# Attention with beacon keys and a low-rank token mixer on one core: the first batch's masks put on TensorE, half of its loads cast by the DMA, its mixing and first products cut into pieces

## The chip, the cores and the metric

The kernel runs on one core of one Trainium2 chip. The metric is the device time of one execution in microseconds (us). A core has TensorE (PE in the profile; its weight loads are PEld), VectorE (DVE), ScalarE (ACT), GpSimd (POOL) and SyncE (SP), which run beside each other and wait for one another by semaphores. DMA transfers are issued from the queues of SP, ACT or POOL.

## The reference, cut to what matters

There are 8 batches of 8 heads, 576 tokens, head size 64, and 16 beacon keys and values per head that every token may see. The output of the attention, 576 x 512 per batch, goes through a low-rank mixing over the tokens (rank 32) and a channel network of width 2048.

```python
k_all = concat([beacon_k, k], axis=2); v_all = concat([beacon_v, v], axis=2)
scores = (q @ k_all^T) / 8                      # q: 8, 8, 576, 64; k_all: 8, 8, 592, 64
scores[t, 16 + s] = -1e9 where s > t            # causal; the 16 beacons are always seen
x = softmax(scores) @ v_all                     # heads laid side by side: 8, 576, 512
u = x + (U @ V mixing over tokens of x)         # h = x^T @ U @ V; u = x + h^T
out = u + relu(u @ w_ch1) @ w_ch2
```

## The kernel before, in words

Heads are worked in pairs: pair p is heads 2c and 2c + 1 of batch b, with p = 4b + c, so pairs 0 to 3 are the first batch. The output tokens of all batches, 4608, are cut into nine blocks of 512 for the channel network.

The program is a list of steps in a string, SCRIPT (L855), that `step` (L791) takes one by one; each engine gets its instructions in that order and takes them strictly in it. The names of the steps that matter here:

- `I1`: one keep-warm matmul of the identity on 128x512 (L241), whose result is not used. `Sa0:3` has three of them ahead of the score step.
- `k`, `q`, `b`, `v`: loads of a batch, or of its half A or B (heads 0 to 3, 4 to 7), issued from POOL (L190 to L204), which cast f32 to f16 on the way. `w10` to `w13` and `w20`, `w21` load the weights of the network in quarters and halves, from POOL too (L180, L185). `u` loads U and V from SP.
- `GkV0`: regroup k (or q) of a pair for the transposes, on V (DVE), A (ACT) or G (POOL) (L253). `HkV0`: copy the first 80 rows of a pair, f32 to f16 (L743). `TqV1`: five transposes on PE and two copies from PSUM (L261 to L265).
- `Sa0` to `Sd0`: the four score groups of a pair. PE multiplies (L316; the two heads of a pair lie in the two halves of the array's rows, 64 each), ACT takes exp (L321).
- `M0.0`, `M0.1`: the mask of a head. DVE takes the minimum of exp and a mask that is 65504 where a key is seen and 0 where it is not (L304, L306). `B` fills the larger mask (L118 to L122).
- `A0.0`: one head's values on PE (L331, 15 matmuls), reciprocal and product on DVE (L339, L340).
- `X0.0` to `X0.2`: the mixing of batch 0 over all four blocks of 128 channels: a head (L371, 20 matmuls, then a copy to f16 on DVE) and two parts (transposes L390, closing matmuls of 32 rows L397, copies on ACT and DVE L406, L408). In the later batches the transposes come from DMA.
- `g0.9`: the first layer of block 0, 128 of its 2048 columns: four matmuls of 512 columns (L529), one for each 128 channels, then relu on ACT, and for the lower half on ACT and DVE (L533 to L539).
- `P02.0` and others: products of the second layer (L620), in an arrangement with seven products per block in place of eight; `p00.0` are sums for them, `W0` sums of weights, `U0.0` transposes by DMA.

All of PSUM is one pool of eight banks (L102), which the steps take in turn. POOL holds the waits for its transfers itself: it issues one after the other.

At the start, `load_first` (L691) brings all of q and k of the first batch as f32 into two staging tiles, pair by pair: pair 0's q from ACT's queue, the rest from SP's. Regroup and head copies then cast to f16. The later batches come by POOL, already cast. The stage that the change touches is the first 200 steps of SCRIPT, up to `X1.0` and `v2`; it holds pairs 0 to 7, the mixing of batch 0, the first layer of block 0, and the start of the second batch's mixing.

Of the kernel before, what the change touches and what calls it, by code (L numbers as in the profile page):

```python
# [27 lines left out]
def kernel(  # L28
# [269 lines left out]
    def score_units(c, qT, kT, ex):  # L298
# [11 lines left out]
        def visit(g, idle=0):  # L310
            ps = [pst([P, 512], F32, name=f"sps{i}") for i in range(2)]
            keep_warm(ps[0], idle)
            for ch, qa, w, o in groups[g]:
                for i in range(2):
                    hp = slice(D * i, D * i + D)
                    nc.tensor.matmul(  # L316
                        ps[i][:, ds(o, w)], kT[hp, c, ds(P * ch, P)], qT[hp, c, ds(qa, w)],
                        start=True, stop=True,
                    )
# [35 lines left out]
    def mix_units(xb, u0, xt=None, shifted=True):  # L355
# [10 lines left out]
        def head():  # L366

            qtp = pst([P, P], F32, name="qtp")
            for m, j in rows:
                for cc in range(NCC):  # L370
# [9 lines left out]
        def part(a, e):  # L380
            n = e - a
            ups = [pst([P, n], F32, name="ups") for _ in range(NCC)]
            if xt is None:
                for cc in range(NCC):
# [10 lines left out]
            for cc in range(NCC):  # L395
# [5 lines left out]
            for cc in range(NCC):  # L401
# [8 lines left out]
        return head, [lambda a=a, e=e: part(a, e) for a, e in zip(cuts, cuts[1:])]  # L410
# [99 lines left out]
    def block_steps(t, dst):  # L510
# [11 lines left out]

        def g_unit(dc):
# [3 lines left out]
            g = pst([P, 512], F32, name="gps")  # L527
            for cc in range(NCC):
                nc.tensor.matmul(  # L529
                    g, w1[:, cc, ts(dc, P)], uT[:, cc, ds(ring(t0), 512)], start=(cc == 0), stop=(cc == NCC - 1)  # L530
                )
# [202 lines left out]
    def group(p, i, copy):  # L734
# [3 lines left out]
        regroup(Ls[b], c, i, copy, prs[p])  # L738
        if b == 0 and not any(t[0] == "H" and t[1] == "kq"[i] and t[3:] == str(p) for t in SCRIPT.split()):
# [51 lines left out]
    def step(t):  # L791
# [7 lines left out]
        elif name in "kqbv":  # L799
# [56 lines left out]
        HqA0 I1 GkA0 I1 I1 I1 GqA0 I1 I1 HkV0 u I1 I1 I1 GkV1 I1 B I1 I1 I1 TqA0 TkA0 I1 TkV1 I1 s v0A  # L856
# [174 lines left out]
```

## Time and profile before

| | |
|---|---|
| median of 3 runs | 339.12 us (338.91 to 340.06) |
| the profiled execution | 339.2 us |
| its span, first to last instruction | 337.5 us |
| mean granted TensorE clock | 0.998 |
| busy: PE, DVE, ACT, POOL | 327.8, 264.8, 228.0, 99.3 us |
| bytes moved by DMA | 44.17 MB, mean 131 GB/s |
| exp on ACT (L321), 256 of them | 111.6 us |
| first-layer matmuls (L529), 384 of them | 91.8 us |
| masks on DVE (L304), 64 of them | 26.7 us |

A row of the timeline or of a group names the line, the engine, the operation, the tiles written and read, the shape and the count; behind the bar or in brackets stands the time that the engine was idle just before, and what released it. The chain of waits is followed back from the last instruction: at each step to what released it, or to the instruction before it on its engine. PE's busy time has modelled ends, so a busy PE says that it had work, not that it ran at its peak.

### The profile page before, as it was taken

How to read it: one execution, taken by the hardware profiler on the slowest of the kernel's cores; microseconds unless marked ns; L12 is line 12 of the kernel's file. 1: busy time of each engine (PE TensorE's matmuls, PEld its weight loads, DVE VectorE, ACT ScalarE, POOL GpSimd, SP SyncE). 2: the span in 40 equal slices, each digit the busy share in tenths (PEclk: the TensorE clock that was granted, in tenths of full speed). 3: DMA queues.
4: the chain of work that ended last, by engine and by line, in shares of the span. 5: the costliest groups of instructions: out<-in, count | busy, mean ns of one | idle time of the engine just before them, and what ended most of it. 6: DMA issues, size and time to landing. Idle time of an engine off the chain costs nothing.

```text
span 337.5 us, 8954 instructions
## 1 busy us (share of the span) xinstructions
PE 327.8 (97%) x3527; PEld 228.0 (68%) x3527; DVE 264.8 (78%) x690; ACT 228.0 (68%) x494; POOL 99.3 (29%) x129
## 2 busy tenths in 40 slices
PE   7989999999999999999999999999999999999994
PEld 3446466765678655766577547765688888888883
DVE  2888588985778757875888868886999999896882
ACT  4897898749778889878785799267912842644500
POOL 9765662340621602450024410000002503303300
PEclk9999999999999999999999999999999999999999
DMA  9999999999999999999979997554545501203042
GB/s 178 221 196 196 153 167 195 98 168 175 164 180 176 169 188 150 124 136 187 189 109 145 172 183 96 83 114 100 51 62 161 93 2 63 80 0 95 3 113 98
DMA packets 136145, 44.17 MB, mean 131 GB/s; under 512 B 108417, under 2 KB 131969, under 8 KB 136097
## 3 DMA queue, kind: packets, MB, share of 16 engines
q0 software_dynamic: 69008, 17.54, 61.3%
q1 hardware_dynamic: 66496, 25.66, 42.0%
q8 instruction: 29, 0.48, 0.6%
q10 hardware_dynamic: 592, 0.34, 0.3%
q14 instruction: 20, 0.16, 0.2%
HBM read 37.63 MB, written 9.44 MB: 139 GB/s over the span
## 4 chain that ended last, share of the span: by engine, by line
PE 75%; DVE 16%; DMA 3%; issue 3%; ACT 2%; SPq 0%; DVEq 0%; ACTq 0%
PE gps L529 23%; PE cpY L620 15%; PE po L331 8%; PE sps L316 8%; PE cpD L620 7%; PE cpA L620 3%; PE fpY L566 3%; DMA stm<-in_q_dram 3%; DVE gT L581 3%; DVE sT L601 2%; DVE ob L645 2%; DVE uT L404 2%; PE fpD L566 2%; PE tps L263 1%; ACT expt L321 1%
## 5 line engine op out<-in xcount | busy, mean ns | idle before, releaser
L321 ACT ACTIVATE expt<-sps 128x496 f16<-128x496 f32 (+2 forms) x256 | 111.6, 538 | 15.8 <-PE sps L316 14.3
L529 PE MATMUL gps<-uT,w 128*128 128x512 f16 x384 | 91.8, 379 | 0.0
L620 PEld LDWEIGHTS <-gT 128*128 128x128 f16 x576 | 54.6, 98 | 10.5 <-issue 2.2
L529 PEld LDWEIGHTS <-w 128*128 128x128 f16 x384 | 34.3, 98 | 37.4 <-issue 2.5
L587 POOL TENSOR_SCALAR gT<-gT 128x512 f16<-128x512 f16 x12 | 17.8, 1495 | 105.6 <-DVE gT L581 89.0
L620 PEld LDWEIGHTS <-sT 128*128 128x128 f16 x432 | 41.0, 98 | 7.8 <-issue 2.0
L331 PEld LDWEIGHTS <-expt 128*128 128x128 f16 (+1 forms) x960 | 35.5, 98 | 9.2 <-DVE expt L304 1.3
L203 POOL DMA_DIRECT2D vs<-in_v_dram x50 | 40.5, 825 | 3.2 <-DMA w<-in_moe_w_ch_dram 2.5
L539 ACT ACTIVATE gT<-gps 128x512 f16<-128x512 f32 x48 | 29.8, 630 | 15.5 <-PE gps L529 15.2
L304 DVE TENSOR_TENSOR expt<-expt,bigmask 128x512 f16<-128x512 f16 x64 | 26.7, 417 | 17.2 <-ACT expt L321 17.2
L331 PE MATMUL po<-vs,expt 128*128 128x65 f16 (+1 forms) x960 | 38.0, 194 | 1.0 <-ACT expt L321 1.0
L620 PE MATMUL cpY<-wsum,gT 128*128 128x256 f16 x288 | 36.1, 273 | 0.0
L620 PE MATMUL cpD<-w,sT 128*128 128x256 f16 x288 | 35.5, 273 | 0.3 <-DVE sT L601 0.3
L316 PE MATMUL sps<-qT,kT 64*128 64x80 f16 (+4 forms) x384 | 34.5, 282 | 0.4 <-ACT kT L109 0.3
L340 DVE TENSOR_TENSOR xb<-po,rec 128x320 f16<-128x320 f32 x64 | 31.5, 492 | 2.2
L534 DVE SCALAR_TENSOR_TENSOR gT<-gps,gT 128x256 f16<-128x256 f32 x48 | 19.8, 420 | 14.9 <-ACT gT L533 14.8
L109 ACT ACTIVATE hP<-fpY 128x512 f32<-128x512 f32 x24 | 13.7, 598 | 23.0 <-PE fpY L566 18.8
L533 ACT ACTIVATE gT<-gps 128x256 f16<-128x256 f32 x48 | 19.5, 418 | 11.5 <-PE gps L529 11.0
L316 PEld LDWEIGHTS <-kT 64*128 64x128 f16 x384 | 13.9, 94 | 18.7 <-issue 10.1
L645 DVE TENSOR_TENSOR ob<-cpY,ut 128x512 f32<-128x512 f32 (+1 forms) x28 | 18.7, 667 | 6.0 <-PE cpY L620 6.0
L566 PEld LDWEIGHTS <-wf 128*128 128x128 f16 x192 | 18.6, 98 | 3.0 <-issue 0.7
L620 PE MATMUL cpY<-w,gT 128*128 128x256 f16 x144 | 17.7, 273 | 0.0
(115 smaller groups left out, 477.6 us busy)
## 6 DMA issues: line engine op xcount, KB each, us to landing
out_dram<-ob SPq DMA_DIRECT2D x16, 512.0 KB, 4.5
st<-in_k_dram POOLq DMA_DIRECT2D x6, 512.0 KB, 8.9
st<-in_q_dram POOLq DMA_DIRECT2D x6, 512.0 KB, 8.6
vs<-in_v_dram POOLq DMA_DIRECT2D x18, 128.0 KB, 7.7
w<-in_moe_w_ch_dram POOLq DMA_DIRECT2D x4, 512.0 KB, 8.6
w<-in_moe_w_ch_dram POOLq DMA_DIRECT2D x2, 1024.0 KB, 12.6
stm<-in_k_dram SPq DMA_DIRECT2D x4, 256.0 KB, 5.0
stm<-in_q_dram SPq DMA_DIRECT2D x3, 256.0 KB, 5.6
```

The source lines that it names most:

```text
L203: nc.gpsimd.dma_start(out=dst[a : a + nq[j], j, :, :], in_=src[hs, ds(q0[j], nq[j]), :].rearrange("h p d -> p h d"))
L304: nc.vector.tensor_tensor(out=e4, in0=e4, in1=bigmask, op=ALU.min)
L316: nc.tensor.matmul(ps[i][:, ds(o, w)], kT[hp, c, ds(P * ch, P)], qT[hp, c, ds(qa, w)], start=True, stop=True,)
L321: nc.scalar.activation(out=ex[i][:, ds(PAD + SLOT * g, gw[g])], in_=ps[i][:, 0 : gw[g]], func=AF.Exp, scale=scale)
L331: nc.tensor.matmul(po[:, j, :], ex[0 : nk[c], ds(blk[(c, j)], P)], vs[0 : nk[c], ds(c * H * E + h * E, E)], start=(c == 0), stop=(c == j),)
L340: nc.vector.tensor_tensor(out=xb[:, h // 2, :, ds(D * (h % 2), D)], in0=po[:, :, 0:D], in1=r.broadcast_to([P, NT, D]), op=ALU.mult)
L529: nc.tensor.matmul(g, w1[:, cc, ts(dc, P)], uT[:, cc, ds(ring(t0), 512)], start=(cc == 0), stop=(cc == NCC - 1))
L534: nc.vector.scalar_tensor_tensor(out=gT[:, dc, H2:512], in0=g[:, H2:512], scalar=0.0, in1=gT[:, dc, 0:H2], op0=ALU.max, op1=ALU.subtract,)
L539: nc.scalar.activation(out=gT[:, dc, :], in_=g, func=AF.Relu)
L566: nc.tensor.matmul(ps[:, i, :], a[:, kk, ts(2 * mp + i, P)], b[:, kk, :], start=opens and i == 0 and kk == 0, stop=kk == 1, skip_group_che ...
L620: nc.tensor.matmul(ps[:, i, :], a[:, f, ds(P * i, P)], b[:, f, :], start=opens and i == 0 and f == 0, stop=f == NK - 1, skip_group_check=True,
L645: nc.vector.tensor_tensor(out=out, in0=ps[:, ii, :], in1=other, op=ALU.add)
```

## The change

The first batch's masks go from DVE to PE. Two operands are filled once at the start (`fill_masks`): `sel` has 65504 times the identity in two halves, `nm` has 0 where a key is seen and -65504 where it is not. Their product, -65504 squared at the masked places, is added to the scores in PSUM ahead of exp, so that exp gives 0 there. The steps `M0` to `M3` go. `B` comes later, since only pairs 4 and up use the old mask.

Pairs 2 and 3 are no longer loaded as f32 by SP: the steps `q0B`, `k0B` and `b0B` load them from POOL as f16, and their head copies go. SP and ACT load pairs 0 and 1.

The mixing of batch 0 is done per block of 128 channels: `D1.0` is the head of block 1, `D1.1` and `D1.2` are its parts. The first-layer products of six column groups are split: `E0.8` does the first three blocks of 128 channels, and `g0.8` the last.

The order of the stage is another. 25 keep-warms stand ahead of the first transpose, where 13 stood; there are 36 in the stage in both. Behind `v2` the list is the same.

```diff
+    msk = outp.tile([P, 2, 2, P], F16, name="msk", tag="ob")
+    sel, nm = msk[:, 0], msk[:, 1]
+    HP = P // 2
+    def fill_masks():
+        nc.vector.memset(sel, 0.0)
+        nc.vector.memset(nm[:, 1, 0:HP], -F16_MAX)
+        nc.vector.memset(nm[:, 0, HP:P], 0.0)
+        for i in range(2):
+            r = slice(HP * i, HP * i + HP)
+            for h in range(2):
+                nc.vector.tensor_scalar(
+                    out=sel[r, h, ds(HP * h, HP)], in0=ident[r, r], scalar1=F16_MAX, scalar2=None, op0=ALU.mult
+                )
+                nc.vector.tensor_scalar(
+                    out=nm[r, h, ds(HP * h, HP)], in0=mask[r, r], scalar1=F16_MAX, scalar2=None, op0=ALU.subtract
+                )
...
-    def score_units(c, qT, kT, ex):
+    def score_units(c, qT, kT, ex, masked=False):
...
-                        start=True, stop=True,
+                        start=True, stop=not masked, skip_group_check=masked,
                     )
+                if masked and qa == q0[ch]:
+                    a = Nb if ch == 0 else 0
+                    for h, e in ((0, HP), (1, min(P, w))):
+                        for i in range(2):
+                            hp = slice(D * i, D * i + D)
+                            nc.tensor.matmul(
+                                ps[i][:, ds(o, e - a)], sel[hp, h, :], nm[hp, h, a:e],
+                                start=False, stop=True, skip_group_check=True,
+                            )
...
-        def head():
+        def head(ccs=range(NCC)):
...
-                for cc in range(NCC):
+                for cc in ccs:
...
-        def part(a, e):
+        def part(a, e, ccs=range(NCC)):
...
+        def g_part(dc, ccs=range(NCC - 1)):
+            if ccs[0] == 0:
+                cell["g", dc] = pst([P, 512], F32, name="gps")
+            for cc in ccs:
+                nc.tensor.matmul(
+                    cell["g", dc], w1[:, cc, ts(dc, P)], uT[:, cc, ds(ring(t0), 512)],
+                    start=(cc == 0), stop=(cc == NCC - 1), skip_group_check=True,
+                )
...
-        main = gtp.tile([P, 2, H, 4 * D], F32, name="stm", tag="gT")
-        head = gtp.tile([P, 2, H, D], F32, name="sth", tag="gT")
+        main = gtp.tile([P, 2, H // 2, 4 * D], F32, name="stm", tag="gT")
+        head = gtp.tile([P, 2, H // 2, D], F32, name="sth", tag="gT")
+        Ls[0] = qk_tiles()
...
+        main_load(nc.scalar, q[0], main[:, 1, SETS[0], :], SETS[0])
+        main_load(nc.sync, k[0], main[:, 0, SETS[0], :], SETS[0])
+        head_load(nc.scalar, q[0], head[:, 1, SETS[0], :], SETS[0], 0)
+        head_load(nc.sync, k[0], head[:, 0, SETS[0], :], SETS[0], Nb)
+        beacon_load(nc.scalar, beacon_k[0], head[:, 0, :, :], HS)
...
-        for hs in SETS[1:]:
-            kload(hs)
-            qload(nc.sync, hs)
+        main_load(nc.sync, k[0], main[:, 0, SETS[1], :], SETS[1])
+        head_load(nc.sync, k[0], head[:, 0, SETS[1], :], SETS[1], Nb)
+        main_load(nc.sync, q[0], main[:, 1, SETS[1], :], SETS[1])
+        head_load(nc.sync, q[0], head[:, 1, SETS[1], :], SETS[1], 0)
...
-        HqA0 I1 GkA0 I1 I1 I1 GqA0 I1 I1 HkV0 u I1 I1 I1 GkV1 I1 B I1 I1 I1 TqA0 TkA0 I1 TkV1 I1 s v0A
-        Sd0 Sb0 Sa0:3 I1 GqV1 TqV1 GkV2 Sc0 I1 GqV2 v0B I1 I1 Sc1 Sb1 I1 M0.0 Sd1 M0.1 TqV2 TkV2 I1 A0.0
...
+        v0A I1 q0B k0B b0B I1 I1 I1 I1 GqA0 q1A I1 I1 I1 I1 I1 I1 GkA1 I1 I1 I1 GkV0 HkV0 I1 I1 HqV0 I1 I1
+        I1 I1 u I1 I1 I1 s I1 I1 TqA0 I1 TkV0 TkV1 Sa0:3 Sb0 Sc0 GqV1 TqV1 I1 cV I1 Sd0 I1 Sa1:2 Sb1 Sc1
+        Sd1 w12 I1 v0B GqV3 eV GqV2 I1 TqA3 GkV2 GkV3 A0.0 TqV2 TkV2 TkA3 A1.0 k2 A0.1 A1.1 I1 GqA5 Sd2 Sb3
+        I1 Sa2:1 Sd3 D1.0 D0.0 D1.2 k1A b1 GqV4 Sc3 Sa3:1 Sc2 Sb2 TqV5 A3.0 D0.1 A3.1 I1 w13 TqA4 A2.0 D1.1
+        D3.0 A2.1 GkA4 D3.2 D0.2 GkV5 D2.0 D3.1 b2 D2.2 k1B GkV11 U0.0 TkV5 TkV4 D2.1 Sb5 Sd5 GkV7 E0.8 Sd4
+        g0.8 q1B g0.11 w10 GkV6 Sb4 Sa5:0 Sc4 Sc5 g0.10 B g0.13 GqV6 E0.9 TqV6 TkV6 I1 I1 v1A GqV7 g0.9
+        TkV11 Sa4 q2 M4.0 E0.0 M4.1 g0.0 GkA8 TkA7 E0.2 U0.2 M5.0 g0.2 g0.12 TkV8 A4.0 A4.1 GqV8 TqA7 A5.0
+        Sa6:0 Sb6 M5.1 Sc6 E0.3 TqV8 U0.1 E0.1 A5.1 Sd6 Sb7 g0.15 GkV10 GqV9 w11 M6.1 g0.1 g0.3 g0.7 GqV11
+        GkV9 M6.0 v1B p00.0 Sa7 Sd7 Sc7 M7.0 g0.14 M7.1 A6.1 g0.6 A6.0 Sc8 Sd8 A7.1 GqV10 A7.0 TkA9 TqA9
+        p00.2 g0.5 p00.1 w20 g0.4 Sd9 Sc9 Sa8 X1.0 w21 TqA11 v2 b3 p01.0 p01.2 X1.1 P02.0 p01.1 X1.2 W0
...
     with tc.manual_schedule(engines={ENG.PE, ENG.Activation, ENG.DVE, ENG.SP, ENG.Pool}):
         load_first()
+        fill_masks()
```

More of the change, by code (lines that the diff above doesn't have):

```diff
@@ L408, in part @@
                     nc.scalar.activation(out=dst, in_=ups[cc], func=AF.Copy)
-        return head, [lambda a=a, e=e: part(a, e) for a, e in zip(cuts, cuts[1:])]
+        return head, [lambda ccs=range(NCC), a=a, e=e: part(a, e, ccs) for a, e in zip(cuts, cuts[1:])]
     def mlp_units(t0, n, dst):
@@ L526, in g_unit @@
             gT = cell["g"]
[L527 to L531, printed above, removed]
+            if ("g", dc) not in cell:
+                g_part(dc, range(NCC))
+            else:
+                g_part(dc, range(NCC - 1, NCC))
+            g = cell["g", dc]
             if dc < NK:
@@ L737, in group @@
             prs[p] = pair_tile()
-        regroup(Ls[b], c, i, copy, prs[p])
-        if b == 0 and not any(t[0] == "H" and t[1] == "kq"[i] and t[3:] == str(p) for t in SCRIPT.split()):
+        regroup((None, raw["main"]) if p < 2 else Ls[b], c, i, copy, prs[p])
+        if p < 2 and not any(t[0] == "H" and t[1] == "kq"[i] and t[3:] == str(p) for t in SCRIPT.split()):
             first_heads(c, i, copy)
```

132 lines of the change are left out of this document (58 added, 74 removed).

## The prediction

> **What bounds the kernel now.** I read the page first, then a table of busy time by stretch, then the chain of waits of the first 62 us, then the timeline of the rows that the change touches.
>
> ```profile
> PE 327.8 (97%) x3527; PEld 228.0 (68%) x3527; DVE 264.8 (78%) x690; ACT 228.0 (68%) x494; POOL 99.3 (29%) x129
> ...
> PE   7989999999999999999999999999999999999994
> ```
>
> TensorE (PE) is busy for 97% of the span. The slices are 8.4 us each: only the first three and the last are under 9 tenths. The change rewrites 200 steps at the head of the order, the part ahead of the step `v2`; from there on both orders are the same word for word. So the question is one number: when does PE reach the end of that part?
>
> The table by stretch has, for each, the length, then the busy time of PE, weight load, DVE, ACT and POOL.
>
> ```profile
> 6.00:12.00 6.00, 5.19 (x51) 2.36 (x48) 4.57 (x21) 5.16 (x14) 5.17 (x9) 1.00 1.58 233
> 12.00:18.00 6.00, 5.72 (x77) 3.00 (x70) 5.49 (x22) 5.14 (x15) 4.69 (x8) 1.00 1.66 212
> 18.00:24.00 6.00, 4.99 (x76) 3.10 (x76) 4.76 (x19) 5.50 (x13) 3.33 (x6) 1.00 1.44 193
> 24.00:30.00 6.00, 5.53 (x80) 3.54 (x79) 5.83 (x20) 4.21 (x11) 4.57 (x7) 1.00 1.34 203
> 30.00:36.00 6.00, 6.00 (x90) 3.61 (x88) 3.88 (x12) 6.00 (x18) 2.40 (x4) 1.00 1.91 170
> 36.00:42.00 6.00, 6.00 (x38) 2.83 (x36) 3.34 (x11) 5.10 (x13) 4.95 (x7) 1.00 1.36 154
> ...
> 120.00:337.50 217.50, 211.99 (x2203) 155.27 (x2200) 174.14 (x409) 131.37 (x270) 39.30 (x40) 1.00 0.77 107
> ```
>
> PE waits only up to 30 us: 0.81 + 0.28 + 1.01 + 0.47 = 2.57 us from 6 to 30. From 30 us on it is full, and behind the stage 212 of 217.5 us. A shift at the end of the stage is therefore carried to the end one for one. DVE is the fullest engine beside PE from 12 to 30.
>
> ```profile
> 0.86 4.27 DMA stm<-in_q_dram
> ...
> 16.84 0.14 PE tps L261
> 16.98 0.23 PE tps L263 x4
> ...
> 28.24 0.22 PE idle L241
> 28.46 0.46 PE po L331 x15
> 28.93 0.32 PE sps L316 x2
> 29.24 0.32 PE idle L241
> ...
> 30.13 0.52 PE qtp L371 x20
> 30.65 0.53 PE ups L390 x8
> 31.18 0.21 PE ups L397 x4
> ...
> 31.70 0.71 PE ups L390 x12
> 32.41 0.25 PE ups L397 x4
> ...
> 33.60 0.32 PE sps L316 x6
> ...
> 35.73 6.15 PE gps L529 x28
> ...
> 43.99 0.97 PE gps L529 x4
> ...
> 46.00 0.86 PE gps L529 x4
> ...
> 59.41 0.98 PE cpA L620 x8
> ```
>
> In the chain (start, length, what) a load of q lies at the head, and behind 28 us there are rows of PE alone. The last row, at 59.41 us, is the first product of `P02.0`, just behind the common point: I take its start as the mark of the stage. The other rows are prices on PE. A transposing step T is 0.14 + 0.23 = 0.37. A keep-warm `I1` is 0.22, or 0.32 behind a score step. A value step A is 0.46, a score step `Sa` or `Sc` 0.32. The run of 28 rows at L529 gives 6.15 / 28 = 0.22 us for 512 columns, or 0.43 ns a column.
>
> **The change, part by part.** All of it is PE time up to the mark, unless I say otherwise.
>
> Keep-warms and start. Both orders have 36 `I1` and the same counts in S steps, but 25 of them now stand ahead of the first transpose, where 13 stood.
>
> ```profile
> 1.59 4.68 PE L241 MATMUL idle<-ident 128*128 128x512 f16 x13 [1.59 <-POOL ident masks.py:199]
> ...
> 4.98 0.80 PEld L241 LDWEIGHTS <-ident 128*128 128x128 f16 x4 [0.28 <-issue]
> ...
> 6.11 0.20 PE L261 MATMUL tps<-ident,hd 80*128 80x80 f16 x1
> ...
> 8.89 5.71 ACT L321 ACTIVATE expt<-sps 128x208 f16<-128x208 f32 x14 [0.35 <-PE sps L316]
> ```
>
> The first eight of the 13 take from 1.59 to 4.98, 0.42 us each; then four weight loads come in 0.80 us, (0.80 - 0.15) / 3 = 0.22 apart. Thirteen end at 6.1, where the first transpose (6.11) starts at once. Twelve more at 0.22 end at 8.7, so `TqA0` starts 2.6 us later. Nothing lets it pass them, since PE takes them in order. The same twelve are gone behind it: -12 x 0.22 = -2.6, or down to -3.2 if half of them stood behind score steps at 0.32. I take 0 in all, and -0.6 as the low end.
>
> Masks by TensorE. For pairs 0 to 3 each score step gets two matmuls per diagonal block and head: in columns, 48 + 112 for the first block, 64 + 128 for three, 64 + 80 for the last, 880 per head. The trace has no such matmul. The nearest is in the score step `Sc`: one 336-column and two 80-column matmuls per head (33.60, six rows) take 0.32, as long as one 496-column matmul per head (28.93, two rows). So the two heads run side by side on their halves of the array, and small matmuls there cost their columns only. That gives 880 x 0.43 = 0.38 a pair, 1.5 us for four; if the heads did not overlap, 3.0. No gain is possible, as nothing leaves PE here. I take 1.5, by the row that is of the same form.
>
> The Trainium skill, page "TensorE: Matmul & The Clock Gate", section "Back-to-back issue gap", would make this dearer: it says that a stream of weight load and matmul pairs is held at about 81 ns a matmul at 128 columns. By it the 80 mask matmuls would be 6.5 us, an estimate, instead of 1.5, and the sum below 5.0 higher. This trace disagrees: 15 matmuls of 65 columns with a weight load each take 0.46 us (28.46), 31 ns apiece.
>
> What the masks take off DVE lies in these groups.
>
> ```profile
> L304 DVE TENSOR_TENSOR expt<-expt,bigmask 128x512 f16<-128x512 f16 x16 | 6.6, 415 | 3.4 <-ACT expt L321 3.4
> ...
> L306 DVE TENSOR_TENSOR expt<-expt,mask 80x80 f16<-80x80 f16 x16 | 3.0, 189 | 0.0
> ...
> L159 DVE COPY one<-ident 32x32 f16<-32x32 f16 x4 | 0.6, 368 | 0.0
> ```
>
> Eight mask steps go, each 0.415 + 0.189: 4.8 us of DVE. They and the lighter regroups (f16 in place of f32) shorten what PE waited for, the 2.57 us; they are worth no more. Added are 11 small DVE instructions that fill the mask operands; by the 32 x 32 copies (0.6 us for four) about 0.15 each, 1.7 us. They lie ahead of the first loaded data (the load in the chain lands at 0.86 + 4.27 = 5.1) and cost nothing; without that cover they would delay the first copy by 1.7. The fill of the old mask moves to where DVE is busy 3.34 of 6 us.
>
> Mixing per channel block. Before, `X0` is a head (20 rows, 0.52) and two parts (0.53 + 0.21, 0.71 + 0.25). Now each is done once per block. Heads: five 128-column matmuls per block; at the 0.23 / 4 of the transposes that is 0.29 a block, 1.15 in all (+0.63), at best +0 if neighbours overlap. The four closing matmuls of a part run side by side before; alone, one of 240 columns is 240 x 0.43 = 0.10 plus what it costs to change the shape of the matmuls. That price shows in the first-layer products: four take 0.86 when value steps follow, 0.97 when 64-row scores follow, so 0.11 a change. Parts: 4 x 0.21 - 0.21 = +0.63 and 4 x 0.25 - 0.25 = +0.75 with the change, +0.20 and +0.33 without. In all +0.5 to +2.0; I take +1.4, since most of these blocks have 128-row neighbours.
>
> First-layer products split. Four of the six split products have other matmuls between their halves, two stand together. The columns are the same; a change of shape more is 0.11 each, 0 to 0.4, and I take 0.1 (only the scores between the halves of `E0.8` change it).
>
> Loads. Pairs 2 and 3 leave SP (eight issues fewer there, which lets the U and V loads go earlier) and are put on POOL, five issues ahead of the next batch's q, of `w12` and of `v0B`; `k2` moves ahead of `k1A`, and waits until pairs 2 and 3 are regrouped and transposed.
>
> ```profile
> 11.59 0.75 POOL L196 DMA_DIRECT2D st<-in_q_dram  x1 [0.83 <-DMA vs<-in_v_dram]
> ...
> 14.59 0.75 POOL L180 DMA_DIRECT2D w<-in_moe_w_ch_dram  x1 [0.25 <-DMA vs<-in_v_dram]
> ...
> 23.65 0.76 POOL L180 DMA_DIRECT2D w<-in_moe_w_ch_dram  x1 [1.61 <-DMA w<-in_moe_w_ch_dram]
> ...
> 37.33 0.76 POOL L180 DMA_DIRECT2D w<-in_moe_w_ch_dram  x1 [0.46 <-issue]
> ```
> ```profile
> w<-in_moe_w_ch_dram POOLq DMA_DIRECT2D x4, 512.0 KB, 8.6
> ...
> vs<-in_v_dram POOLq DMA_DIRECT2D x12, 64.0 KB, 7.3
> ```
>
> From the 13th issue (11.59) to the 25th (23.65) POOL needs 1.0 us each, and the row at 23.65 shows why: it waits for the weight load of 14.59, eight issues before. So five more issues are 5 us. `v0B` ends as the 20th, 11.59 + 7 = 18.6, plus 7.3 to land is 25.9; its first user, `A3.0`, comes at about 26. The last first-layer weights (`w11`) go from 37.33 to 42.3, plus 8.6 is 50.9. Its first user `g0.7` stands ahead of the mark by five g (0.9), eight S (0.28), four A, three T, and `X1` (0.4 + 0.74): 4.5 + 2.2 + 1.8 + 1.1 + 1.1 = 10.7. With the mark at 60.6 that is 49.9: possibly 1.0 late. I price the loads at 0 in the sum, 1.0 as the other end.
>
> Waits that stay. The sum so far is 0 + 1.5 + 1.4 + 0.1 = +3.0, against 2.57 us of waits that could all go: +0.4. How many stay? ACT sets the second limit. The first exp starts at 8.89 before. Now `TqA0`, `I1` and `TkV0` end at 8.7 + 0.37 + 0.22 + 0.37 = 9.6, the copies on DVE about 0.9 later, the score step 0.32 behind them: 10.9. The 14 exps from 8.89 run without a gap, 5.71 / 14 = 0.41 each; 32 of them are 13.1, with three copies of some 0.7 between them 15.2. So the last exp of pairs 0 to 3 is out at 26.1 at the earliest. PE then has about 4.4 us (two A, two T, two heads and six parts of the mixing) to the end of the mixing, and what followed that before, 59.41 - 32.66 = 26.75, plus 1.4 for work that stood ahead of it before (one T, four S) and 0.1: 26.1 + 32.7 = 58.8. PE alone gives 59.8, ACT alone 58.8. Two queues so close to full, joined by eight PSUM banks, reach neither; I keep a third of the old waits, 0.8, with 0 and 2.0 as ends.
>
> Sum: +3.0 - 2.57 + 0.8 = +1.2 us. The profiled execution took 339.2 (span 337.5 and 1.7 around it), against a median of 339.12; I count from 339.2 and get 340.4. With all low ends it is -0.6 + 1.5 + 0.5 - 2.57 = -1.2, with the high end of the mixing, of the split and of the waits +0.4 + 0.6 + 0.3 + 1.2 = +2.5 (masks at 1.5).
>
> **The rivals.** (1) No net effect: DVE was what made PE wait, and with its masks gone PE runs through. For it: 5.49 and 5.83 of 6 us in the table. Against: the first exp comes 2 us later. Time: between the +0.4 of the sum with no waits left and nothing, +0.2: 339.4. (2) Faster: as (1), and the mixing per block overlaps (+0.5, not +1.4) and the keep-warms that went were the 0.32 ones. That is the sum of low ends, -1.2: 338.0. It decides if the closing matmuls run at 0.10 each. (3) POOL late: the five issues put `w11` and the second half of v behind their users; PE waits 1.0 at `g0.7` and some 0.4 earlier. On top of the forecast: 341.8. It decides if `w11` is issued after 41. (4) The masks cost a price per matmul and not per column: at the 0.23 / 4 = 0.058 of a 128-column transpose, 80 of them are 4.6 instead of 1.5, 3.1 on top of the forecast: 343.5. The 31 ns of the value steps leave it little. The Trainium skill's page named above has such a price, and with its estimate of 6.5 the time would be 345.4.
>
> **How the numbers follow.** This kernel's runs lie within about 0.3% (1.0 us), so less than that is "same". Forecast 0.50, of which 0.15 lies under +1.0; rival (1) 0.18; (2) 0.15; (3) 0.14; (4) 0.03. Slower: 0.35 + 0.14 + 0.03 = 0.52; same 0.15 + 0.18 = 0.33; faster 0.15. The predicted time is that of the forecast, 340.4, on its own from 339.6 to 341.7. The range goes from rival (2), 338.0, to 1.0 beyond rival (3), 342.8; half of (2), (4) and a tail of (3) are outside, about 0.15.
>
> **What would show it.** First transpose at 8.7, first exp near 10.9. A mask matmul pair at the pace of its columns: a score group with masks 0.07 to 0.14 longer than without. DVE well under 5 us of 6 between 12 and 30. PE waits of some 0.8 between 9 and 32. Closing matmuls of the mixing at 0.2 each. `w11` issued near 42. The mark, the first product of `P02.0`, at about 60.6. It is wrong if PE starts its first transpose well before 8.7, if the mark is at 59 or less, or if the time changes behind the mark, where the order is the same.

## The result: slower by 0.6%

The changed kernel takes 341.01 us (median of 13 runs), the kernel before 339.12 (13 runs beside it): a ratio of 1.0058, with a 95% interval of 1.0036 to 1.0080. The profiled execution took 341.23 us, its span is 339.5.

The mark of the prediction, the first product of `P02.0`, is read from the view of that product's tile: behind the count come the least, median and largest duration, then the first and the last start. First the kernel before, then the changed one.

```profile
L620 PE MATMUL cpA<-w,gT x16: 272/273/282, 59.3 to 64.8; 128*128 128x256 f16 x16
```
```profile
L658 PE MATMUL cpA<-w,gT x16: 272/273/283, 61.4 to 66.9; 128*128 128x256 f16 x16
```

59.3 became 61.4: 2.1 us, and the two profiled executions differ by 2.0. Behind the mark nothing is added; the shift is carried to the end. It arises ahead of it. From the timelines of the engines of the changed kernel, each row with its start and duration: weight loads of the keep-warms, the first transpose, the first exp.

```profile
4.98 0.15 PEld L260 LDWEIGHTS <-ident 128*128 128x128 f16 x1 [0.27 <-issue]
...
6.26 0.15 PEld L260 LDWEIGHTS <-ident 128*128 128x128 f16 x1 [0.27 <-issue]
6.69 2.51 PEld L260 LDWEIGHTS <-ident 128*128 128x128 f16 x12 [0.28 <-issue]
```
```profile
9.53 0.20 PE L280 MATMUL tps<-ident,hd 80*128 80x80 f16 x1
```
```profile
11.82 4.34 ACT L349 ACTIVATE expt<-sps 128x496 f16<-128x496 f32 x10 [1.11 <-PE sps L344]
```

The loads come 0.43 us apart up to 6.69, and only the last twelve at 0.22. In the kernel before the pace doubled at 4.98. So the 25 keep-warms end at 9.5, not 8.7, and the first exp starts at 11.82, not 10.9. The table by stretch, in the columns of before:

```profile
6.00:12.00 6.00, 6.00 (x49) 3.01 (x48) 1.81 (x11) 1.72 (x5) 5.30 (x9) 1.00 1.70 199
12.00:18.00 6.00, 5.43 (x89) 3.19 (x82) 3.68 (x12) 6.00 (x15) 5.72 (x8) 1.00 1.44 176
18.00:24.00 6.00, 5.87 (x124) 4.24 (x120) 5.19 (x18) 5.20 (x17) 3.85 (x7) 1.00 1.68 162
24.00:30.00 6.00, 5.96 (x116) 4.32 (x115) 4.06 (x14) 5.24 (x12) 4.75 (x8) 1.00 1.40 177
...
120.00:337.50 217.50, 213.99 (x2216) 156.14 (x2214) 175.03 (x412) 133.34 (x276) 39.40 (x40) 1.00 0.76 108
```

PE waits 0 + 0.57 + 0.13 + 0.04 = 0.74 us from 6 to 30, where it was 2.57; up to 9.5 it has the keep-warms to do. DVE is busy for 3.68, 5.19 and 4.06 us from 12 to 30, 12.93 in all, where it was 5.49 + 4.76 + 5.83 = 16.08. So DVE does have less to do, and PE runs nearly without a gap. PE starts its work 3.4 us later and gets 1.3 us of that back; the run b_front below bears on what gives it back. Then the chain of waits up to the mark:

```profile
1.59 8.10 PE idle L260 x25
...
11.71 0.12 PE sps L344 x4
11.83 5.24 ACT expt L349 x12
...
20.80 0.09 PE sps L344 x4
...
24.60 0.07 PE sps L344 x4
...
24.82 0.08 PE sps L344 x4
...
24.98 0.07 PE sps L344 x4
...
25.24 0.09 PE sps L344 x4
...
26.33 0.20 PE ups L426
...
29.53 0.31 PE ups L426
...
30.10 0.24 PE ups L426
30.34 0.39 PE qtp L399 x5
...
36.25 3.76 ACT expt L349 x8
...
46.78 2.44 ACT expt L349 x5
```

The chain begins with 25 keep-warms, 8.10 us, where before it began with a load. L344 is a mask's four matmuls, 0.07 to 0.13. L426 is a closing matmul of the mixing, alone, L399 a head. From 33 to 49 us rows of ACT (exp) and of DVE now stand in it, where PE alone stood. The chain of the kernel before has one more row near its start that matters here:

```profile
6.67 5.58 DMA stm<-in_q_dram
```

This second load of q, pair 1's, lands at 12.25, and the chain goes on from it. The first transpose at 6.11 is not on that chain, so a first transpose that comes 3.4 us later need not cost 3.4 us.

### The profile page after: what moved, and what is told of

It reads as the page before. It is cut to its first block, busy times and chain, and to the rows that moved or that the text cites. A ratio compares the mean times of both kernels' runs of the same rounds, so it can differ in the third digit from the quotient of the medians.

```text
span 339.5 us, 9106 instructions
## 1 busy us (share of the span) xinstructions
PE 331.0 (97%) x3607; PEld 231.4 (68%) x3607; DVE 262.4 (77%) x685; ACT 227.2 (67%) x493; POOL 103.1 (30%) x134
## 4 chain that ended last, share of the span: by engine, by line
PE 72%; DVE 16%; ACT 7%; issue 3%; POOL 0%; DVEq 0%; ACTq 0%; POOLq 0%
PE gps L556 20%; PE cpY L658 15%; PE cpD L658 7%; PE po L359 7%; PE sps L335 6%; ACT expt L349 5%; PE cpA L658 3%; PE fpY L604 3%; DVE gT L619 3%; PE idle L260 3%; DVE sT L639 2%; DVE ob L683 2%; DVE uT L433 2%; PE fpD L604 2%; PE ups L426 1%
## 5 line engine op out<-in xcount | busy, mean ns | idle before, releaser
L335 PE MATMUL sps<-qT,kT 64*128 64x80 f16 (+4 forms) x384 | 33.8, 281 | 0.4 <-DVE kT L284 0.3
L323 DVE TENSOR_TENSOR expt<-expt,bigmask 128x512 f16<-128x512 f16 x56 | 23.4, 418 | 13.9 <-ACT expt L349 13.9
```

The source lines that it names most:

```text
L323: nc.vector.tensor_tensor(out=e4, in0=e4, in1=bigmask, op=ALU.min)
L335: nc.tensor.matmul(ps[i][:, ds(o, w)], kT[hp, c, ds(P * ch, P)], qT[hp, c, ds(qa, w)], start=True, stop=not masked, skip_group_check=masked,)
```

## The experiments

All are compared with the kernel before on the same chip. "First T" is the first transpose, "mark" the first product of `P02.0`, both in us in the run's own profile.

| run | first T | first exp | mark | median us | ratio to before (95%) |
|---|---|---|---|---|---|
| kernel before | 6.11 | 8.89 | 59.3 | 339.12 | 1 |
| changed kernel | 9.53 | 11.82 | 61.4 | 341.01 | 1.0058 (1.0036 to 1.0080) |
| lead13 | 6.42 | 9.27 | 59.2 | 338.92 | 0.9990 (0.9966 to 1.0014) |
| x_whole | 9.13 | 11.42 | 61.1 | 340.62 | 1.0031 (1.0009 to 1.0053) |
| masks_dve | 9.07 | 11.29 | 69.8 | 349.08 | 1.0276 (1.0254 to 1.0298) |
| b_front | 9.93 | 12.08 | 61.3 | 340.53 | 1.0033 (1.0020 to 1.0047) |
| loads_f32 | 9.84 | 12.13 | 68.8 | 348.49 | 1.0246 (1.0207 to 1.0285) |
| b_masks | 6.78 | 9.01 | 59.2 | 339.14 | 0.9997 (0.9975 to 1.0018) |
| early | 6.97 | 9.26 | 60.0 | 339.37 | 1.0005 (0.9979 to 1.0032) |
| lead13_x | 6.34 | 9.13 | 58.8 | 338.92 | 0.9989 (0.9964 to 1.0013) |
| b_no | 6.15 | 8.38 | 59.3 | 339.79 | 1.0013 (0.9995 to 1.0030) |
| b_masks_no | 7.11 | 9.45 | 57.2 | 336.93 | 0.9923 (0.9897 to 0.9949) |
| lead13_no | 6.32 | 9.56 | 58.6 | 337.99 | 0.9960 (0.9939 to 0.9981) |
| loads_u | 9.21 | 11.50 | 64.6 | 344.34 | 1.0147 (1.0121 to 1.0173) |

The theory was that of the prediction: the stage is a full queue of PE, with ACT close behind; the later start costs, the masks and pieces cost PE time, and the relief of DVE pays some of it back. The rivals: the keep-warms in front are the whole loss; the POOL loads set the pace; the pieces of the mixing lie in waits.

**lead13.** Twelve of the 25 keep-warms in front taken out.

```diff
-        v0A I1 q0B k0B b0B I1 I1 I1 I1 GqA0 q1A I1 I1 I1 I1 I1 I1 GkA1 I1 I1 I1 GkV0 HkV0 I1 I1 HqV0 I1 I1
-        I1 I1 u I1 I1 I1 s I1 I1 TqA0 I1 TkV0 TkV1 Sa0:3 Sb0 Sc0 GqV1 TqV1 I1 cV I1 Sd0 I1 Sa1:2 Sb1 Sc1
+        v0A I1 q0B k0B b0B I1 I1 I1 I1 GqA0 q1A I1 I1 I1 I1 I1 I1 GkA1 I1 I1 GkV0 HkV0 HqV0
+        u s TqA0 I1 TkV0 TkV1 Sa0:3 Sb0 Sc0 GqV1 TqV1 I1 cV I1 Sd0 I1 Sa1:2 Sb1 Sc1
```

> The changed kernel with 12 of the 25 keep-warms ahead of the first transpose taken out, so 13 as before; nothing else. My theory: the stage behind the first transpose is a full queue of PE and ACT, so an earlier start comes through: first transpose at 6.2 to 7 us in place of 9.7, first exp near 9.2 in place of 11.8 (the copy of k of pair 1 on ACT, done at 8.0, sets it), the mark (first product of P02.0, 61.5 in the changed kernel) near 59, and a time about 2.0 under the 341.0 of the changed kernel, 339.0. Rival (the loads set the pace of the stage, POOL above all): the mark stays within 0.7 of 61.5, and the time at 340.5 to 341.

The chain of waits of lead13, start and duration ahead of each row:

```profile
2.19 4.67 DMA stm<-in_k_dram
...
7.42 0.30 ACT hd L109
...
9.28 1.96 ACT expt L349 x4
```

The median is 338.92, 2.1 under the changed kernel, and no longer to be told from the kernel before. In the chain a load (2.19 + 4.67 = 6.9) and its copies on ACT (to 7.7) hold the first score step, no keep-warm. First T comes 3.1 us earlier than in the changed kernel, the mark 2.2. So the stage does follow its start, with 0.9 lost on the way, and the loads that POOL issues, the same as in the changed kernel, do not set its pace.

**b_front.** The other direction: in the kernel before, the first twelve keep-warms behind `TqA0` moved ahead of it.

```diff
-        HqA0 I1 GkA0 I1 I1 I1 GqA0 I1 I1 HkV0 u I1 I1 I1 GkV1 I1 B I1 I1 I1 TqA0 TkA0 I1 TkV1 I1 s v0A
-        Sd0 Sb0 Sa0:3 I1 GqV1 TqV1 GkV2 Sc0 I1 GqV2 v0B I1 I1 Sc1 Sb1 I1 M0.0 Sd1 M0.1 TqV2 TkV2 I1 A0.0
...
+        HqA0 I1 GkA0 I1 I1 I1 GqA0 I1 I1 HkV0 u I1 I1 I1 GkV1 I1 B I1 I1 I1 I1 I1 I1 I1 I1 I1 I1 I1 I1 I1 I1
+        I1 TqA0 TkA0 TkV1 s v0A Sd0 Sb0 Sa0:3 GqV1 TqV1 GkV2 Sc0 GqV2 v0B Sc1 Sb1 M0.0 Sd1 M0.1 TqV2 TkV2
...
```

> The kernel before with only its keep-warms moved: 25 ahead of the first transpose in place of 13, and the first 12 behind it taken out. My theory as predicted: -2.6 and +2.6 cancel on PE, but the later first exp (about 11.5 in place of 8.9) takes waits of PE behind it with it, so between 0 and +2.0; I say +1.3, 340.4. Rival (the 25 in front alone are the whole loss): +1.9 or more, 341.0. Second rival (the keep-warms behind the start sat where PE waited for DVE anyway, so taking them out gains nothing): +2.6, 341.7.

340.53, a ratio of 1.0033, or 1.1 us. First T is 3.8 us later, the mark 2.0. So by the keep-warms alone more than half of the loss appears in the kernel before; its interval reaches neither the changed kernel's estimate nor nothing.

Here too 1.8 of the 3.8 us come back, with the masks still on DVE. In the table by stretch cut at first T and at the mark, PE works for 50.63 of 53.19 us in the kernel before, 47.53 of 51.37 in b_front and 50.45 of 51.87 in the changed kernel. So moving the keep-warms takes 3.1 us of work out of the stretch behind first T and adds 1.3 us of waits to it. The rest of the change adds 2.9 us of work and takes 2.4 us of waits away. Whether these waits go because DVE has less to do, or because the added work fills them, these runs do not separate.

**x_whole and lead13_x.** The mixing of batch 0 whole again, at the place of the last block's pieces, in the changed kernel and in lead13.

```diff
-        I1 Sa2:1 Sd3 D1.0 D0.0 D1.2 k1A b1 GqV4 Sc3 Sa3:1 Sc2 Sb2 TqV5 A3.0 D0.1 A3.1 I1 w13 TqA4 A2.0 D1.1
-        D3.0 A2.1 GkA4 D3.2 D0.2 GkV5 D2.0 D3.1 b2 D2.2 k1B GkV11 U0.0 TkV5 TkV4 D2.1 Sb5 Sd5 GkV7 E0.8 Sd4
+        I1 Sa2:1 Sd3 k1A b1 GqV4 Sc3 Sa3:1 Sc2 Sb2 TqV5 A3.0 A3.1 I1 w13 TqA4 A2.0
+        A2.1 GkA4 GkV5 X0.0 b2 X0.2 k1B GkV11 TkV5 TkV4 X0.1 U0.0 Sb5 Sd5 GkV7 E0.8 Sd4
```

> The changed kernel with the mixing of batch 0 done for all four channel blocks at once, as before, at the place of the last block's pieces (the DMA turn U0.0 goes behind it); the keep-warms, masks, loads and split products stay. My theory: the mixing per block costs PE 1.2 us (closing matmuls of 0.20 to 0.31 each in the changed kernel's chain, heads of 0.39), so the mark comes 1 us earlier and the time is 340.0. Rival (the pieces fill time in which PE waits for ACT and DVE anyway, and the late whole mixing puts copies of all blocks in a row): the mark is the same or up to 1 us later, time 341 to 342.

> The changed kernel with 12 keep-warms fewer in front and the mixing of batch 0 whole, as in the run x_whole. My theory after x_whole (its mark, counted from the first transpose, was no earlier, as the copies of the mixing and the sums of the value steps on DVE then stand in the chain): the mixing per block is neutral, 338.9 as lead13, within 0.7. Rival (per block it costs PE 1.2, which shows once the start is early): 337.9.

The chain of waits of x_whole, then its table by stretch:

```profile
27.77 0.49 DVE xb L368
...
28.94 0.46 PE qtp L399 x18
...
30.43 0.91 DVE uT L435 x2
...
32.95 0.33 DVE uT L435
```
```profile
24.00:30.00 6.00, 4.39 (x105) 3.65 (x103) 3.83 (x12) 4.45 (x11) 3.65 (x6) 1.00 1.42 182
30.00:36.00 6.00, 5.08 (x55) 2.43 (x54) 4.18 (x17) 4.59 (x13) 4.13 (x6) 1.00 1.80 179
```

The whole head takes 0.46 us where the pieces took 0.47 + 0.39 + 0.39, so PE does save; but it waits 1.61 us from 24 to 30 and 0.92 from 30 to 36, since the products of the last values (DVE, 27.77) and the copies of all blocks (30.43, 32.95) now stand in a row. The median is 0.4 under the changed kernel, with intervals that overlap; counted from first T the mark is no earlier (52.0 against 51.9): between the two PE works 2.2 us less (48.26 against 50.45) and waits 2.3 us more. In lead13_x it is the same as in lead13, 338.92 twice. The pieces are neutral: they cost PE and fill its waits.

**masks_dve.** In the changed kernel, the masks of the first batch back on DVE, right ahead of the value steps.

```diff
-            scs[p] = score_units(c, qT_of(b), kTs[b % 2], ex_of(p), b == 0)
+            scs[p] = score_units(c, qT_of(b), kTs[b % 2], ex_of(p), False)
...
-        I1 I1 u I1 I1 I1 s I1 I1 TqA0 I1 TkV0 TkV1 Sa0:3 Sb0 Sc0 GqV1 TqV1 I1 cV I1 Sd0 I1 Sa1:2 Sb1 Sc1
-        Sd1 w12 I1 v0B GqV3 eV GqV2 I1 TqA3 GkV2 GkV3 A0.0 TqV2 TkV2 TkA3 A1.0 k2 A0.1 A1.1 I1 GqA5 Sd2 Sb3
...
+        I1 I1 u B I1 I1 I1 s I1 I1 TqA0 I1 TkV0 TkV1 Sa0:3 Sb0 Sc0 GqV1 TqV1 I1 cV I1 Sd0 I1 Sa1:2 Sb1 Sc1
+        Sd1 w12 I1 v0B GqV3 eV M0.0 M0.1 GqV2 I1 TqA3 GkV2 GkV3 M1.0 M1.1 A0.0 TqV2 TkV2 TkA3 A1.0 k2 A0.1
...
```

> The changed kernel with the first batch's masks back on DVE (eight mask steps put back ahead of the value steps that use them, the score matmuls unmasked, the larger mask filled at the start while DVE is idle; the filling of the two operands stays and is unused). My theory: PE loses 80 small matmuls, 0.41 us a pair by the changed kernel's chain, 1.6 in all, and DVE, busy 3.7, 5.2 and 4.1 of 6 us from 12 to 30, takes 3.6 to 4.8 us back; where PE is the longer queue the mark comes 0.5 to 1.5 earlier: 340.0. Rival (DVE's masks are what PE waited for in the kernel before): the value steps wait for them, the mark is 0.5 to 1.5 later: 342.

The table by stretch of masks_dve, then the largest row of its waits of PE from 12 to 30 us (total, times, longest):

```profile
12.00:18.00 6.00, 4.92 (x50) 2.43 (x51) 3.85 (x15) 6.00 (x17) 5.24 (x8) 1.00 1.53 180
18.00:24.00 6.00, 4.74 (x84) 3.04 (x84) 5.29 (x20) 4.23 (x12) 5.08 (x8) 1.00 1.69 174
24.00:30.00 6.00, 3.95 (x61) 2.51 (x62) 3.56 (x13) 4.61 (x12) 4.60 (x8) 0.98 1.43 191
30.00:36.00 6.00, 4.75 (x50) 3.13 (x48) 3.79 (x13) 1.23 (x3) 4.01 (x6) 0.50 1.69 177
36.00:42.00 6.00, 6.00 (x35) 2.72 (x34) 4.01 (x12) 2.75 (x7) 5.42 (x8) 0.50 1.47 189
```
```profile
PE po L359 <- DVE expt L323: 2.3, 3, 1.2
```

349.08: both expectations fail by size, though the rival's wait of the value steps for the masks is there. The last three columns are the granted clock, the DMA share and the rate. PE waits 1.08, 1.26 and 2.05 us of 6, 2.3 in all for L323, the masks on DVE, and from 30 to 42 the granted clock is 0.50: 4.75 + 6.00 us of PE at half pace, by estimate some 5.4 us lost. So the price of the masks alone can't be read from this, all the less as the order was made for masks on PE.

**b_masks, b_no and b_masks_no.** So the same part was tried in the order of before: masks on PE, then the 23 keep-warms behind the first transpose taken out, without and with the masks on PE. (The 13 in front and those inside score steps stay.)

```diff
-        HqA0 I1 GkA0 I1 I1 I1 GqA0 I1 I1 HkV0 u I1 I1 I1 GkV1 I1 B I1 I1 I1 TqA0 TkA0 I1 TkV1 I1 s v0A
-        Sd0 Sb0 Sa0:3 I1 GqV1 TqV1 GkV2 Sc0 I1 GqV2 v0B I1 I1 Sc1 Sb1 I1 M0.0 Sd1 M0.1 TqV2 TkV2 I1 A0.0
...
+        HqA0 I1 GkA0 I1 I1 I1 GqA0 I1 I1 HkV0 u I1 I1 I1 GkV1 I1 B I1 I1 I1 TqA0 TkA0 TkV1 s v0A Sd0 Sb0
+        Sa0:3 GqV1 TqV1 GkV2 Sc0 GqV2 v0B Sc1 Sb1 Sd1 TqV2 TkV2 A0.0 GqV3 Sa1:2 A0.1 Sd2 GkV3 q1A Sc2 TqA3
...
```

This is b_masks_no; b_masks keeps the `I1`, b_no keeps the `M` and the masks on DVE.

> The kernel before with its own order, loads and keep-warms, and only the first batch's masks on PE: the eight mask steps taken out, the masked score matmuls in. My theory as predicted: +1.6 on PE against at most 2.57 us of waits: between -1.0 and +1.0, 339.2. Rival (in that order PE waits for DVE, whose masks stand right ahead of the value steps; the masks on PE take those waits away wholly): -1.5, 337.8. Second rival (no wait goes, as ACT sets those places): +1.6, 341.0.

> The kernel before (masks on DVE) with the 23 keep-warms of the stage behind the first transpose taken out; the 13 in front and those inside score steps stay. My theory: in that order PE waits for ACT and DVE between 6 and 30 us, and the keep-warms fill such waits, so taking them out gives little: mark within 1.0 of 59.3, time 338.7 to 339.4. Rival (they are on the path, 23 x 0.22 = 5 us of PE): mark 55 to 57, time 335 to 337. Second rival (PE's clock drops in the longer waits): 341 or more, the granted clock under 1 in the table by stretch.

> The run b_masks (kernel before, first batch's masks on PE) with the same 23 keep-warms taken out. In b_masks PE is busy 6.00 of 6 us from 12 to 24 and waits only 0.6 from 6 to 30, with the keep-warms counted as work. My theory: there the keep-warms are part of PE's full queue, so taking them out gives what ACT and DVE leave free: mark 57.5 to 58.5, time 337.5 to 338.5, under the kernel before; so masks on PE pay only together with fewer keep-warms. Rival (ACT sets the stage in both): 339.0, as b_masks. Second rival (the clock drops): 341 or more.

The tables by stretch of b_masks, b_no and b_masks_no in this order, and the mark of the last:

```profile
12.00:18.00 6.00, 6.00 (x106) 3.89 (x107) 4.94 (x16) 4.86 (x13) 4.88 (x8) 1.00 1.66 208
18.00:24.00 6.00, 6.00 (x106) 3.81 (x102) 3.39 (x12) 5.49 (x14) 3.28 (x6) 1.00 1.44 195
```
```profile
12.00:18.00 6.00, 4.62 (x70) 2.92 (x71) 5.84 (x22) 5.34 (x15) 4.17 (x7) 1.00 1.70 201
18.00:24.00 6.00, 4.10 (x66) 2.66 (x64) 4.89 (x19) 4.63 (x12) 3.84 (x6) 0.85 1.43 193
24.00:30.00 6.00, 5.94 (x80) 4.64 (x82) 5.62 (x19) 3.88 (x11) 4.46 (x7) 0.58 1.34 202
```
```profile
12.00:18.00 6.00, 5.61 (x113) 3.88 (x114) 4.94 (x17) 5.81 (x16) 4.59 (x8) 1.00 1.64 204
18.00:24.00 6.00, 4.83 (x96) 3.37 (x95) 4.63 (x16) 6.00 (x16) 3.43 (x6) 1.00 1.44 197
```
```profile
L658 PE MATMUL cpA<-w,gT x16: 272/273/283, 57.2 to 62.6; 128*128 128x256 f16 x16
```

Masks on PE alone change nothing (0.9997): PE, with its keep-warms, is busy 6.00 of 6 us in two stretches, so the waits of before became work. Taking the keep-warms out alone gains nothing either (1.0013): PE then waits 1.38 and 1.90 us, DVE stays at 5.84 and 5.62, and the granted clock falls to 0.85 and 0.58. At these clocks 4.10 and 5.94 us of PE's work lose some 0.15 x 4.10 + 0.42 x 5.94 = 3.1 us, by estimate; how much of what the keep-warms would give is held back by the masks on DVE, and how much by the clock, is not separated. Both together give 0.9923 (0.9897 to 0.9949), 2.3 us under the kernel before, with the mark at 57.2 and the clock at 1.00. This is the version that beats both kernels: the order of before, its loads and its whole mixing, the masks on PE, and 23 keep-warms fewer. Its chain of waits begins with loads that POOL issues: the beacon keys of the second batch, asked for at 16.35, land 7.41 us later, at 23.8, and PE's transposes wait for them. What would be gained there was not tried.

**lead13_no.** lead13 without the eleven keep-warms behind the first transpose.

```diff
-        v0A I1 q0B k0B b0B I1 I1 I1 I1 GqA0 q1A I1 I1 I1 I1 I1 I1 GkA1 I1 I1 GkV0 HkV0 HqV0 u s TqA0 I1 TkV0
-        TkV1 Sa0:3 Sb0 Sc0 GqV1 TqV1 I1 cV I1 Sd0 I1 Sa1:2 Sb1 Sc1 Sd1 w12 I1 v0B GqV3 eV GqV2 I1 TqA3 GkV2
...
+        v0A I1 q0B k0B b0B I1 I1 I1 I1 GqA0 q1A I1 I1 I1 I1 I1 I1 GkA1 I1 I1 GkV0 HkV0 HqV0 u s TqA0 TkV0
+        TkV1 Sa0:3 Sb0 Sc0 GqV1 TqV1 cV Sd0 Sa1:2 Sb1 Sc1 Sd1 w12 v0B GqV3 eV GqV2 TqA3 GkV2 GkV3 A0.0 TqV2
...
```

> The run lead13 (changed kernel with 13 keep-warms in front) with the 11 keep-warms behind the first transpose taken out too; the change as it stands, without what it has too much. My theory: PE waits in lead13 for DVE and ACT already (1.2 us from 6 to 24), so the 11 x 0.22 = 2.4 give at most half: 338.0 to 338.9. Rival (on the path): 336.5.

337.99, 0.9960 (0.9939 to 0.9981), as the theory had it: the change as it stands beats the kernel before once its surplus keep-warms are gone, but by less than b_masks_no, whose interval overlaps. Its chain, too, runs through POOL's loads, to a k of the second batch that lands at 22.60 + 8.50 = 31.1.

**early.** lead13 with the regroup of pair 1's k (`GkA1`) moved behind the first copies of q on ACT, and the first score block of pair 0 ahead of `TkV1`.

```diff
-        v0A I1 q0B k0B b0B I1 I1 I1 I1 GqA0 q1A I1 I1 I1 I1 I1 I1 GkA1 I1 I1 GkV0 HkV0 HqV0 u s TqA0 I1 TkV0
-        TkV1 Sa0:3 Sb0 Sc0 GqV1 TqV1 I1 cV I1 Sd0 I1 Sa1:2 Sb1 Sc1 Sd1 w12 I1 v0B GqV3 eV GqV2 I1 TqA3 GkV2
+        v0A I1 q0B k0B b0B I1 I1 I1 I1 GqA0 q1A I1 I1 I1 I1 I1 I1 I1 I1 GkV0 HkV0 HqV0 u s TqA0 GkA1 I1 TkV0
+        Sa0:3 TkV1 Sb0 Sc0 GqV1 TqV1 I1 cV I1 Sd0 I1 Sa1:2 Sb1 Sc1 Sd1 w12 I1 v0B GqV3 eV GqV2 I1 TqA3 GkV2
```

> The changed kernel with 12 keep-warms fewer in front, as in the run lead13, and the regroup of k of pair 1 moved behind the first copies of q on ACT, its transposes behind the first score step, so that the first exp no longer waits for pair 1's load (chain of lead13: that load ends at 6.9, regroup and head copy on ACT to 7.7). My theory: first exp near 8.5 in place of 9.3, and the stage behind it follows by most of that: mark 58.5, time 338.3, under both kernels. Rival (behind the start DVE and PE set the pace in lead13, which its chain shows from 13.7 to 20 us): no change against lead13, 338.9.

It failed: the first exp is at 9.26 as in lead13, first T in this profile at 6.97 and not 6.42, and 339.37 is not under lead13. In this profile nearly all of the 13 keep-warms run at the slow pace, so whether the copies on ACT hold the start stays open.

**loads_f32 and loads_u.** The changed kernel with the first loads as before; in loads_u also with the casts of U and V later.

```diff
-        v0A I1 q0B k0B b0B I1 I1 I1 I1 GqA0 q1A I1 I1 I1 I1 I1 I1 GkA1 I1 I1 I1 GkV0 HkV0 I1 I1 HqV0 I1 I1
+        v0A I1 I1 I1 I1 I1 GqA0 q1A I1 I1 I1 I1 I1 I1 GkA1 I1 I1 I1 GkV0 HkV0 I1 I1 HqV0 I1 I1
...
-        main_load(nc.sync, k[0], main[:, 0, SETS[1], :], SETS[1])
-        head_load(nc.sync, k[0], head[:, 0, SETS[1], :], SETS[1], Nb)
+        for hs in SETS[1:]:
+            kload(hs)
+            qload(nc.sync, hs)
...
-        I1 Sa2:1 Sd3 D1.0 D0.0 D1.2
+        I1 Sa2:1 Sd3 cV eV D1.0 D0.0 D1.2
```

The last pair of lines is in loads_u alone.

> The changed kernel with the first loads as before: all four pairs come as f32 from SP and ACT, and the three steps that load pairs 2 and 3 from POOL are taken out, so POOL issues five transfers fewer; masks, mixing, split products and the order stay. My theory (the loads cost nothing in the sum): within 0.7 of the changed kernel, 340.5 to 341.5, as ACT and PE set the stage; the regroups in f32 cost DVE some 0.15 each and four head copies 0.2 each, at places where it has room. Rival (POOL late): the weights and the second batch come earlier and PE's 0.6 us of waits behind 30 us go: 340.0 or less. Rival (f16 loads are the gain in the change): 342.

> The run loads_f32 again (changed kernel, all four first pairs as f32 from SP and ACT, five POOL issues fewer), but with the casts of U and V and the spreading of V moved from ahead of pair 2's regroups to just ahead of the mixing. In loads_f32 the loads of U and V came behind the f32 loads in SP's queue, V landed at 21.0, and DVE, which takes its steps in order, stood at the cast from 15 to 21, with PE's clock at 0.68 to 0.75. My theory: with the cast out of the way the f16 loads are worth nothing by themselves: 340.5 to 341.5. Rival (the rest of loads_f32's 8 us is the later regroup and the lost clock): 343 or more. Second rival (POOL's five issues cost PE its waits behind 30 us): 340.0 or less.

A row of the chain and two of the table by stretch of loads_f32, then a row of the chain of loads_u:

```profile
12.81 8.18 DMA small<-in_moe_V_dram
```
```profile
18.00:24.00 6.00, 2.48 (x25) 1.74 (x26) 3.35 (x13) 1.50 (x5) 1.43 (x2) 0.75 1.80 183
24.00:30.00 6.00, 6.00 (x95) 4.96 (x94) 4.26 (x14) 2.66 (x8) 4.61 (x8) 0.68 0.62 67
```
```profile
9.34 8.69 DMA sth<-in_q_dram
```

In loads_f32 the loads of U and V stand behind the f32 loads in SP's queue: V is issued at 12.81, where it was at 6.62 in the changed kernel, and lands at 12.81 + 8.18 = 21.0. DVE waits 6.1 us for U and 0.2 for V at their casts, PE has 2.48 of 6 us of work, and the clock falls. The queue alone does not do it: in the kernel before V is issued at 12.62, but its cast stands later in the order, at 21.9, and nothing waits there. In loads_u, with the casts later, the time is 344.34, some 4 less; now the last head load of q, at 9.34 + 8.69 = 18.0, holds DVE. So in the changed order the f16 loads through POOL are worth 3 us or more, lost clock included (0.72 from 18 to 24 in loads_u), against my "nothing". That does not price them in another order: b_masks_no, the fastest of all, has f32 loads.

The split products were not tried alone.

## Why the prediction was right, step by step

The direction, slower, was right, and so was the picture of the stage: a PE with almost no waits left and ACT close behind. The size, 1.2 us forecast and 1.9 measured (339.12 to 341.01), came near in part by luck, since it was added up from other terms than those that made it. The keep-warms, put at 0, cost 1.1 when moved alone (b_front), and with the twelve in front taken out the whole loss is gone (lead13). The mixing, put at +1.4, is worth nothing measurable, with 25 keep-warms in front (x_whole) or with 13 (lead13_x). The masks' 1.5 is there as work on PE, but in the order of before it all went into waits (b_masks).

**The start** was mis-sized. Forecast was a first transpose at 8.7 and 2.6 us of delay. The cost of a warm keep-warm was read rightly (0.22), but it was taken for granted that the slow phase ends at 4.98, as in the one profile at hand. Over the runs with 13 keep-warms in front, first T was at 6.11, 6.42, 6.78, 6.97, 6.34, 6.15, 7.11 and 6.32 (mean 6.52), over those with 25 at 9.53, 9.13, 9.07, 9.93, 9.84 and 9.21 (mean 9.45). The mean delay is 2.93, and the profile of before had the earliest start of eight. (In lead13, lead13_x and lead13_no it is a fill on DVE, L168, and not the last keep-warm that releases the first transpose, so the mean is not of the keep-warms alone.) The Trainium skill, page "TensorE: Matmul & The Clock Gate", section "The HAM clock gate (the 'warmup' mystery)", says that the slow phase is a span of time in a window that runs by itself, so that its end varies by about 0.5 us from run to run. By that rule a single profile does not give the start. These runs agree on the varying, but with more of it: full pace came between 4.53 us (lead13_no) and 7.54 (b_front) over these fourteen profiles.

**The twelve keep-warms gone behind**, forecast at -2.6, and **the waits**, forecast to fall from 2.57 to 0.8, belong together. From first T to the mark the forecast was 60.6 - 8.7 = 51.9 us, down from 53.2; measured is 61.4 - 9.5 = 51.9. The sum behind the start was right, but two errors of 0.6 cancel in it: PE worked for 50.45 us, where the forecast comes to 50.63 + 0.4 = 51.0, and waited for 1.42, where it has 0.8. The runs in the order of before show that the two were not to be had one by one: keep-warms out alone 1.0013 (with the clock lost), masks off DVE alone 0.9997, both 0.9923.

**The masks**: forecast 0.38 a pair, by columns. The five groups of a pair can be read in the chain from pairs 2 and 3: 0.09 for `Sd` (20.80), 0.07 for `Sa` (24.60), 0.08 and 0.07 for `Sc` (24.82, 24.98) and 0.09 for `Sb` (25.24), 0.40 in all. By rival (4), at 0.058 a matmul, a group of four would be 0.23; it is out.

**The mixing** was sized too low on PE and did not matter: heads 0.47 + 0.39 + 0.39 = 1.25 (forecast 1.15), closing matmuls of 0.20 and 0.24 to 0.31, the dearer end of the forecast, which took +1.4 out of a range to +2.0. But x_whole and lead13_x show that PE's price is not the kernel's.

**The loads**, rival (3), failed: `w11` was forecast at 42.3. From the timeline of POOL of the changed kernel:

```profile
37.91 0.76 POOL L199 DMA_DIRECT2D w<-in_moe_w_ch_dram  x1
```

It is issued at 37.91, 0.6 later than before. Five more issues cost 0.6 in all: the 1.0 an issue of before was a mean over twelve, with POOL's waits for single transfers in it, and no price of an issue. **Rivals (1) and (2)** failed at the start: PE did run nearly without waits, but from 9.53 on; rival (2) also at its own condition, as closing matmuls took 0.20 and more and not 0.10. lead13 and lead13_no, which start early, come to where they put the time (339 and 338), but by another way: they have 12 and 23 keep-warms fewer than the change.

Two readings in the prediction are wrong without moving its forecast. Its high end adds 1.2 us of waits to the sum without any, where its own high end for them is 2.0, so it is +3.3 and not +2.5, and the forecast's own range goes to 342.5 and not 341.7. And of the 40 slices of PE the first, the third and the last are under 9 tenths; the second is not. One more of its signs failed: DVE was to be well under 5 us of 6, and was at 5.19 from 18 to 24.

What stays open: the 0.4 us between the forecast with the mean start (1.2 + 0.3) and the measured 1.9 is less than the interval, and isn't assigned.

## What to carry to other kernels

Filler work that keeps a clock up was free here only while its engine waited for others. When a change takes that waiting away, count the filler as work, and try to take it out in the same step: masks off DVE gained nothing until 23 keep-warms went too, and those, which alone also cost the clock, gained nothing until the masks were off DVE. Filler ahead of the first real step was a delay that the later steps did not give back in full (3.8 us at the start, 2.0 at the mark in b_front); end it when the first data has landed.

## What the runs showed that was not expected

The granted clock fell to 0.50 (masks_dve, 30 to 42 us) and 0.58 (b_no, 24 to 30) though PE was at work for 3.95 to 4.74 us of every 6 in the 12 us before; a clock so lost cost several us, by the estimates above. In b_masks_no PE worked 4.83 to 5.61 of 6 from 12 to 30, and it stayed at 1.00; it also did behind a single stretch of 4.29 in lead13_x (24 to 30). What decides it is not shown. The column of granted clock reads 1.00 also for 0 to 6 us, where the keep-warms run at half pace: the pace of the weight loads shows the slow start, that column does not. And eight more loads ahead in SP's queue made the small loads of U and V land as late as 21.0, and since DVE takes its steps in order, the whole kernel stood behind their casts: the changed kernel with f32 loads took 7.5 us more (348.49 against 341.01), lost clock included, and some 4 of these went when only the casts and the spreading of V were moved back (loads_u).
